# Beacon attention and low-rank mixer: every step of the script in another order, with score column groups in longer stretches

## The chip, the cores and the metric

The kernel runs on one core of one Trainium2 chip. The metric is the device time of one execution in microseconds (us), as the median of the runs. Three runs of the kernel before took 339.13, 339.48 and 340.19 us, with 339.48 us as the median.

## The reference

For 8 batches of 8 heads, 576 queries of 64 numbers attend to 16 beacon keys and to 576 keys under a causal mask. The heads are put side by side to 512 channels, and a mixer follows: a rank-32 product over the tokens, added to its input, and a two-layer ReLU network of 2,048 hidden channels, added again.

```python
k_all = np.concatenate([beacon_k, k], axis=2)
scores = scale * np.matmul(q, k_all.transpose(0, 1, 3, 2))
scores = np.where(causal, -1000000000.0, scores)
a = np.exp(scores - scores.max(-1, keepdims=True))
a /= a.sum(-1, keepdims=True) + 1e-09
x = np.matmul(a, v_all)                # then (batch, token, head * 64)
h = xt @ U @ V                         # xt: x with tokens last
u = x + h.transpose(0, 2, 1)
out = u + np.maximum(u @ w_ch1, 0.0) @ w_ch2
```

## The kernel before

The program is one straight list of steps. A string, SCRIPT, names them; `step` (a chain of comparisons on the first letter) turns each name into instructions, and every engine runs its instructions in exactly the order in which the script issues them. Nothing reorders them later: TensorE (PE), VectorE (DVE), ScalarE (ACT), GpSimd (POOL) and the DMA queues of SP and POOL each hold their own list, and only semaphores tie the lists together. So the order of the 961 names is the whole schedule.

Work is cut in pairs of heads, 32 of them, four for each batch. The steps of pair p are these, where a letter A or V after the name says whether ACT or DVE makes the copy:

- `k`, `q`, `b`, `v` and `w` issue the loads on POOL's queue. `H` and `G` regroup a loaded piece into a tile `pr` (L253 on DVE, L109 on ACT).
- `T` turns queries or keys so that the 64 numbers of a head lie along the partitions. In the first three batches PE does it (L261, L263, into PSUM) and a copy brings it to `qT` or `kT` (L109 on ACT, L264 and L265 on DVE). From pair 12 on, `R` issues the transposition as a DMA on SP's queue (tile `raw`, L283), and `T` is only the copy out of it.
- `Sa`, `Sb`, `Sc`, `Sd` are the four score column groups of a pair. Each has matmuls on 64 rows of the array, the two heads on the two halves (L316), and two exponentials on ACT (L321) that empty the two PSUM banks into `expt`. Group a is 496 columns wide, b 464, c 496 in three pieces, d 208. The number after a colon adds matmuls without use, which keep the array busy.
- `M` masks one head on DVE (L304, L306). `A` multiplies it with the values (15 matmuls, L331, tile `po`), then DVE divides by the row sums into `xb` (L339, L340). Four `expt` tiles hold two pairs at a time.
- `X` is the mixer's low-rank part for a batch: `X.0` works on 32-column tiles of the array (L371, then a copy on DVE, L377), `X.1` and `X.2` end in matmuls on 32 rows (L397). `x` issues DMA transpositions of `xb` that the later batches need for it.
- `g` is one of 16 first-layer units of a 512-token block (four matmuls of 512 columns, L529, evacuated by ACT at L533 and DVE at L534, or by ACT alone at L539). `p`, `P`, `F`, `V`, `N`, `W` and `U` make the two layers out of products of sums of blocks (L620 and L566 on PE, L601, L581 and L645 on DVE), and write the output.
- `I1` is one 512-column matmul without use (L241), 37 in all. `Z16` and `Z18` are one-element copies on POOL (L822) that read the DMA-transposed tile of pair 16 or 18: as POOL runs in order, the loads behind them are issued only when that tile has landed.

All PSUM tiles are taken in turn from one pool of 8 banks, so a new tile waits until an older one has been emptied by ACT or DVE. PE has three shapes of the array in this program besides the full one: 64 rows (`S`), 32 rows (end of `X.1` and `X.2`, and once in `e`), and 32 columns (`X.0`).

Of the kernel before, what the change touches and what calls it, by code (L numbers as in the profile page):

```python
# [27 lines left out]
def kernel(  # L28
# [760 lines left out]
    def step(t):  # L789
# [70 lines left out]
        GkV11 g0.1 M5.0 g0.10 g0.0 GkV8 g0.14 q2 g0.3 g0.11 GkA9 A5.0 A5.1 Sb7 I1 w11 TkV8 GqV8 GqV9 Sa7  # L860
        g0.2 M4.0 GqV11 Sd7 Sc7 TkV11 TkA9 g0.8 A4.1 M7.0 TqA9 A4.0 p00.0 p00.1 Sb6 v1B Sa6:0 g0.12
        p00.2 TqV11 M7.1 Sc6 g0.4 Sd6 g0.15 M6.0 GkA10 w20 U0.1 M6.1 TqV8 g0.6 A7.1 A7.0 Sd9 Sc9 w21
        A6.1 g0.7 A6.0 Sd8 g0.5 Sc8 Sa8 GqV10 X1.0 v2 b3 p01.0 p01.2 X1.1 P02.0 p01.1 X1.2 W0 P01.0 Sb8
        W4 W5 W1 Sb9 Sa9 W2 U1.1 W6 P01.1 TkA10 P02.1 M8.1 M9.0 TqA10 W7 b4 M8.0 U0.3 P05.0 P05.1 q3
        P06.0 P06.1 M9.1 A8.1 A9.0 A8.0 Sa10 P03.0 P03.1 k3 g1.15 A9.1 q4 Sa11 Sd10 g1.5 g1.1 Sb10 Sc10
        g1.3 g1.2 GkV13 GqA12 M10.0 GkA12 W3 P07.0 M10.1 P07.1 GqA13 Sb11 Sd11 GqA14 Sc11 M11.1 g1.9
        M11.0 GkA14 g1.12 A10.0 g1.7 g1.10 g1.0 R12 R13 R14 g1.6 TkV12 TqV12 TkV13 P04.0 GqA16 A11.1
        g1.8 U1.0 U1.3 TqA13 GkA15 P04.1 g1.14 A11.0 k4 A10.1 Sa13 Sd12 g1.11 p10.0 g1.4 GqA17 g1.13
        Sa12 Sb12 Sc12 p11.0 GqV15 X2.0 M12.0 P11.0 GkA17 P11.1 U1.2 X2.1 GkV16 p11.1 R15 P12.0 P12.1
        R16 P16.0 TqV14 Sd13 Sb13 M12.1 p10.1 p10.2 Sc13 P16.1 b5 U2.2 M13.0 TkA14 v3 A12.1 q5 A12.0 R17  # L870
        GkA19 P15.0 P15.1 p11.2 Sa14 Sd14 Sc14 x12 P17.0 TkV15 M13.1 P13.0 U2.3 A13.0 Sb14 Z16 M14.0
        P17.1 P13.1 GqA19 GqA18 TkV16 TqA16 A13.1 g2.13 g2.10 TqV17 TqV15 M14.1 v4 g2.4 Sa15 k5 Sc15
        TkA17 P14.0 A14.0 P14.1 A14.1 Sd16 GqV20 Sb15 Sd15 M15.1 GkV18 g2.0 x14 Sc16 M15.0 g2.7 g2.5
# [5 lines left out]
        GkV23 TkV20 TkA21 R22 b7 A19.1 g3.7 A19.0 R23 g3.13 g3.8 g3.5 Sa21 Sb21 Sc21 P24.0 P24.1 A18.1
        A18.0 Sb20 U3.3 Sd21 Sa20 M21.1 M21.0 g3.3 g3.2 Sc20 Sd20 X4.0 g3.4 M20.0 k6 GkV24 M20.1 g3.15  # L880
        GqA26 N5 v5 TkV22 g3.12 A21.0 U3.1 A20.0 g3.10 N1 GkA26 g3.1 x17 q7 g3.0 A20.1 TqV22 TqA23 TkV23
        g3.6 g3.14 g3.9 p30.0 p30.2 A21.1 Sc23 GkV25 p31.0 Sb23 GqV25 Sa23 R24 p30.1 x18 P31.0 P31.1
        GkV27 P32.0 P32.1 TkA24 p31.1 Sc22 p31.2 U3.2 k7 Sd22 v6 Sa22 P36.0 P36.1 Sb22 x19 M22.1 Sd23
        M23.0 P35.0 R25 R26 M22.0 P35.1 X4.1 P37.0 P37.1 X4.2 GqV27 TqA24 TqA25 P33.0 U4.1 P33.1 TkA25
        P34.0 R27 g4.0 GqV28 A22.1 TkV26 GkA28 R28 M23.1 g4.11 GqV29 g4.2 g4.6 TqV26 A23.0 g4.10 A23.1
        Sd25 Sc25 A22.0 g4.4 GkV29 R29 Sb25 GkV30 Sa25 M25.0 Sd24 TqV27 P34.1 TkA27 g4.3 U4.3 TkV28
        M25.1 g4.15 g4.13 g4.9 Sc24 Sa24 x21 Sb24 M24.0 U4.2 X5.0 A25.0 M24.1 g4.8 g4.12 U4.0 GqV31 x22
        g4.1 p40.0 p40.1 GqA30 A25.1 g4.7 Sa27 Sb27 A24.1 g4.14 A24.0 g4.5 p41.0 GkV31 Sc27 x23 Sc26
        p41.2 p41.1 Sd26 P41.0 P41.1 Sa26 Sd27 M27.1 Sb26 P45.0 p40.2 P42.0 P42.1 P45.1 TkA29 x20 X5.1
        U5.3 A27.1 R30 TqV29 M27.0 P46.0 P46.1 P43.0 P43.1 g5.13 A27.0 M26.0 M26.1 Sd29 g5.11 X5.2 g5.4  # L890
        U5.1 TqV28 P47.0 g5.2 A26.1 TkA30 x27 P47.1 A26.0 N0 Sb29 Sc29 R31 N4 g5.6 N2 Sb28 Sa29 g5.0 x24
        P44.0 g5.15 TqA30 M29.1 P44.1 x25 Sd28 Sa28 v7 Sc28 M28.1 M28.0 A29.1 g5.7 g5.14 TkV31 g5.1 g5.5
        M29.0 A28.0 g5.3 N3 A28.1 Sb30 TqV31 Sa30 g5.10 A29.0 U5.0 g5.12 g5.9 x29 g5.8 N6 p51.0 p51.2
        X6.0 p50.0 Sb31 Sd30 p50.1 x26 p51.1 Sc31 P51.0 P51.1 Sd31 p50.2 Sc30 M30.0 M30.1 Sa31 M31.0 x28
        U5.2 P52.0 M31.1 P56.0 X6.1 P55.0 A31.1 V6.0 U6.1 V6.2 P56.1 A31.0 x31 P52.1 A30.1 A30.0 V6.1
        x30 P57.0 P55.1 P57.1 X6.2 X7.0 N7 P53.0 P53.1 U6.2 F61.3 X7.2 P54.0 P54.1 F62.3 F61.2 X7.1
        F66.3 F62.2 F61.0 F65.0 V6.3 F65.3 V7.0 F62.0 U7.2 F66.2 F65.1 F67.3 F63.3 F61.1 F66.0 F62.1
        F63.0 F64.3 F66.1 F65.2 F67.2 F71.3 F67.0 F75.0 F67.1 F63.1 U7.0 F71.0 V7.1 F64.0 U7.3 F63.2
        p61.0 V8.0 P61.0 V7.3 F64.2 F64.1 F76.0 F76.3 U7.1 p61.1 U6.3 p60.0 p60.1 p60.2 U6.0 P61.1 P62.0
        P62.1 P65.0 p61.2 P65.1 guard V7.2 P66.0 P66.1 P63.0 P63.1 F75.3 F72.0 F72.3 F75.2 F77.0 F73.0  # L900
        P67.0 P67.1 F73.3 F71.1 F71.2 F72.1 F72.2 F76.1 F76.2 F75.1 V8.2 V8.1 P64.0 P64.1 F77.1 F77.2
        V8.3 F81.0 F74.0 F73.1 F74.1 U8.2 F77.3 p70.0 p70.2 F74.2 sum F73.2 p71.0 P71.0 p70.1 F74.3
        p71.2 F85.1 p71.1 F81.1 P71.1 P72.0 P72.1 F85.3 P75.0 P75.1 P76.0 P76.1 P73.0 P73.1 F82.1 U8.1
# [125 lines left out]
```

## Time and profile before

| | |
|---|---|
| median of 3 runs | 339.48 us |
| the profiled execution, span | 338.5 us |
| PE busy | 328.5 us of 338.5 |
| DVE busy | 264.9 us |
| ACT busy | 227.9 us |
| POOL busy | 99.8 us |
| matmuls on PE | 3,527 |

The span is the time from the first to the last instruction of one profiled execution; it lies 0.9 us below the median of the runs. Starts are given from the beginning of the span. In lists of instructions the columns are start, length, engine, source line, operation, tile written and tile read, shapes and a count; a pair of square brackets tells how long the engine stood idle before, and what ended that. A matmul's length includes the time in which it runs through the array, so its neighbours overlap with it; what one costs PE is read from the distance between starts.

### The profile page before, as it was taken

Reading aid. Unit: us, or ns where it says so; the run is one execution under the profiler, and the core shown is the slowest. Engines: PE = TensorE matmul, PEld = TensorE weight load, DVE = VectorE, ACT = ScalarE, POOL = GpSimd, SP = SyncE. Lnnn points to the kernel's source line nnn. Section 1 sums busy time; section 2 is a strip of 40 time slices with the busy share of each in tenths; the row PEclk is TensorE's granted clock in tenths of the full one; section 3 lists DMA queues with packets and bytes.
Section 4 is the critical chain, followed back from the end, with each engine's and each line's share of the span. In section 5 each row is a group of like instructions: output and inputs, shape, how many; then the busy total and the mean of one; then the engine's idle time right before and its main releaser. Section 6 shows DMA issues by size and latency. Waiting matters only on the chain.

```text
span 338.5 us, 8950 instructions
## 1 busy us (share of the span) xinstructions
PE 328.5 (97%) x3527; PEld 228.3 (67%) x3527; DVE 264.9 (78%) x690; ACT 227.9 (67%) x494; POOL 99.8 (29%) x129
## 2 busy tenths in 40 slices
...
GB/s 177 221 195 194 126 155 198 134 162 171 168 191 170 167 190 147 114 154 189 171 117 132 179 151 134 68 128 100 48 64 159 95 2 63 80 0 95 5 79 129
DMA packets 135600, 44.17 MB, mean 130 GB/s; under 512 B 108384, under 2 KB 130912, under 8 KB 135552
## 3 DMA queue, kind: packets, MB, share of 16 engines
...
q14 instruction: 19, 0.16, 0.2%
...
## 4 chain that ended last, share of the span: by engine, by line
PE 69%; DVE 17%; DMA 6%; issue 3%; ACT 2%; SPq 1%; DVEq 0%; ACTq 0%
PE gps L529 21%; PE cpY L620 14%; PE cpD L620 7%; PE po L331 7%; PE sps L316 7%; DMA stm<-in_q_dram 4%; PE cpA L620 3%; PE fpY L566 3%; DVE gT L581 3%; DMA raw<-pr 3%; DVE ob L645 2%; DVE sT L601 2%; DVE uT L404 2%; PE fpD L566 2%; DVE xb L340 1%
## 5 line engine op out<-in xcount | busy, mean ns | idle before, releaser
L321 ACT ACTIVATE expt<-sps 128x496 f16<-128x496 f32 (+2 forms) x256 | 111.6, 538 | 16.1 <-PE sps L316 14.7
L529 PE MATMUL gps<-uT,w 128*128 128x512 f16 x384 | 91.8, 379 | 0.3 <-DVE ob L645 0.3
L620 PEld LDWEIGHTS <-gT 128*128 128x128 f16 x576 | 54.6, 98 | 10.5 <-issue 2.2
L529 PEld LDWEIGHTS <-w 128*128 128x128 f16 x384 | 34.4, 98 | 37.5 <-issue 2.5
L587 POOL TENSOR_SCALAR gT<-gT 128x512 f16<-128x512 f16 x12 | 17.8, 1495 | 105.6 <-DVE gT L581 89.0
L620 PEld LDWEIGHTS <-sT 128*128 128x128 f16 x432 | 40.9, 98 | 7.9 <-issue 2.0
L203 POOL DMA_DIRECT2D vs<-in_v_dram x50 | 40.6, 824 | 4.9 <-DMA w<-in_moe_w_ch_dram 2.5
L331 PEld LDWEIGHTS <-expt 128*128 128x128 f16 (+1 forms) x960 | 35.5, 98 | 9.5 <-DVE expt L304 1.5
L539 ACT ACTIVATE gT<-gps 128x512 f16<-128x512 f32 x48 | 29.7, 628 | 15.7 <-PE gps L529 15.2
L304 DVE TENSOR_TENSOR expt<-expt,bigmask 128x512 f16<-128x512 f16 x64 | 26.7, 418 | 17.1 <-ACT expt L321 17.1
L331 PE MATMUL po<-vs,expt 128*128 128x65 f16 (+1 forms) x960 | 38.1, 194 | 1.2 <-DVE expt L304 1.2
L620 PE MATMUL cpY<-wsum,gT 128*128 128x256 f16 x288 | 36.1, 273 | 0.0
L620 PE MATMUL cpD<-w,sT 128*128 128x256 f16 x288 | 35.5, 273 | 0.3 <-DVE sT L601 0.3
L316 PE MATMUL sps<-qT,kT 64*128 64x80 f16 (+4 forms) x384 | 34.6, 282 | 0.5 <-ACT kT L109 0.5
L340 DVE TENSOR_TENSOR xb<-po,rec 128x320 f16<-128x320 f32 x64 | 31.5, 492 | 2.2
L534 DVE SCALAR_TENSOR_TENSOR gT<-gps,gT 128x256 f16<-128x256 f32 x48 | 19.8, 420 | 15.1 <-ACT gT L533 14.9
L109 ACT ACTIVATE hP<-fpY 128x512 f32<-128x512 f32 x24 | 13.7, 598 | 23.0 <-PE fpY L566 18.8
L533 ACT ACTIVATE gT<-gps 128x256 f16<-128x256 f32 x48 | 19.4, 415 | 11.5 <-PE gps L529 11.0
L316 PEld LDWEIGHTS <-kT 64*128 64x128 f16 x384 | 14.0, 94 | 18.9 <-issue 10.1
L645 DVE TENSOR_TENSOR ob<-cpY,ut 128x512 f32<-128x512 f32 (+1 forms) x28 | 18.7, 667 | 6.0 <-PE cpY L620 6.0
L566 PEld LDWEIGHTS <-wf 128*128 128x128 f16 x192 | 18.6, 98 | 2.9 <-issue 0.7
L620 PE MATMUL cpY<-w,gT 128*128 128x256 f16 x144 | 17.7, 273 | 0.0
...
## 6 DMA issues: line engine op xcount, KB each, us to landing
...
```

Source lines behind the costliest of these rows:

```text
L203: nc.gpsimd.dma_start(out=dst[a : a + nq[j], j, :, :], in_=src[hs, ds(q0[j], nq[j]), :].rearrange("h p d -> p h d"))
L304: nc.vector.tensor_tensor(out=e4, in0=e4, in1=bigmask, op=ALU.min)
L316: nc.tensor.matmul(ps[i][:, ds(o, w)], kT[hp, c, ds(P * ch, P)], qT[hp, c, ds(qa, w)], start=True, stop=True,)
L321: nc.scalar.activation(out=ex[i][:, ds(PAD + SLOT * g, gw[g])], in_=ps[i][:, 0 : gw[g]], func=AF.Exp, scale=scale)
L331: nc.tensor.matmul(po[:, j, :], ex[0 : nk[c], ds(blk[(c, j)], P)], vs[0 : nk[c], ds(c * H * E + h * E, E)], start=(c == 0), stop=(c == j),)
L340: nc.vector.tensor_tensor(out=xb[:, h // 2, :, ds(D * (h % 2), D)], in0=po[:, :, 0:D], in1=r.broadcast_to([P, NT, D]), op=ALU.mult)
L529: nc.tensor.matmul(g, w1[:, cc, ts(dc, P)], uT[:, cc, ds(ring(t0), 512)], start=(cc == 0), stop=(cc == NCC - 1))
L534: nc.vector.scalar_tensor_tensor(out=gT[:, dc, H2:512], in0=g[:, H2:512], scalar=0.0, in1=gT[:, dc, 0:H2], op0=ALU.max, op1=ALU.subtract,)
L539: nc.scalar.activation(out=gT[:, dc, :], in_=g, func=AF.Relu)
L566: nc.tensor.matmul(ps[:, i, :], a[:, kk, ts(2 * mp + i, P)], b[:, kk, :], start=opens and i == 0 and kk == 0, stop=kk == 1, skip_group_che ...
L620: nc.tensor.matmul(ps[:, i, :], a[:, f, ds(P * i, P)], b[:, f, :], start=opens and i == 0 and f == 0, stop=f == NK - 1, skip_group_check=True,
L645: nc.vector.tensor_tensor(out=out, in0=ps[:, ii, :], in1=other, op=ALU.add)
```

## The change

The multiset of steps is the same, and so is all code outside the string. The names stand in another order. The steps that issue loads on POOL's queue keep their order among themselves, and so do those that issue transfers on SP's queue. `Z16` and `Z18` are not among those kept: `Z16` stood ahead of `v4` and `k5` and now stands behind them, `Z18` stood ahead of `q6`, `b7`, `k6` and `v5` and now stands behind them. Of the 37 `I1`, 13 stood ahead of the first `T`, and 20 do now.

```diff
     SCRIPT = """
-        HqA0 I1 GkA0 I1 I1 I1 GqA0 I1 I1 HkV0 u I1 I1 I1 GkV1 I1 B I1 I1 I1 TqA0 TkA0 I1 TkV1 I1 s v0A
-        Sd0 Sb0 Sa0:3 I1 GqV1 TqV1 GkV2 Sc0 I1 GqV2 v0B I1 I1 Sc1 Sb1 I1 M0.0 Sd1 M0.1 TqV2 TkV2 I1 A0.0
...
-        A1.1 Sd3 Sa3:1 w12 I1 Sb3 cV M2.1 GqV4 A2.1 b1 k1B TqV4 GkA5 Sc3 I1 GkV4 I1 M3.0 q1B eA GqV5
-        TkV4 I1 GkV7 TkA5 I1 w13 A2.0 Sd4 M3.1 I1 TqV5 A3.0 GkA6 b2 w10 I1 A3.1 k2 Sa4 I1 Sd5 GqV6 GqV7
-        TkA7 X0.0 X0.1 Sa5:0 X0.2 Sb4 TqV7 TqV6 Sc5 TkA6 v1A g0.9 Sc4 M4.1 Sb5 M5.1 U0.0 U0.2 g0.13
...
-        g2.2 A15.0 A15.1 x13 Sd17 Sb17 g2.9 U2.0 X3.0 b6 Sa16 X2.2 g2.3 x15 Sa17 Sb16 R18 R19 Z18 GkV20
-        M16.1 Sc17 M17.1 M17.0 g2.1 g2.6 g2.12 M16.0 g2.8 g2.15 A17.0 U2.1 TqA19 GqA21 TqA18 X3.1 A16.1
...
+        I1 I1 HkV0 I1 u I1 I1 v0A I1 I1 GkV1 v0B I1 I1 s I1 HqA0 B I1 I1 I1 I1 GqA0 I1 I1 GqV1 GkA0 q1A I1
+        I1 I1 I1 TqA0 k1A w12 TkA0 b1 TkV1 I1 I1 Sa0:3 I1 Sc0 Sd0 Sb0 I1 TqV1 I1 M0.0 I1 k1B GkV2 I1 Sd1
+        Sa1:2 M0.1 GqV2 TkV2 I1 Sc1 Sb1 TqV2 A0.1 M1.1 A0.0 I1 Sc2 q1B Sd2 Sa2:1 M1.0 GqV3 I1 GkV3 Sb2 GqV5
+        I1 GqV4 I1 I1 TqA3 M2.0 TkV3 I1 I1 M2.1 I1 A1.0 A1.1 Sc3 Sd3 TqV5 Sa3:1 Sb3 GkA5 cV w13 I1 A2.0
+        GkV4 A2.1 eA M3.1 b2 M3.0 TkA5 TkV4 TqV4 GkA6 GkV7 A3.0 TkA6 GqV6 A3.1 Sa4 Sa5:0 w10 k2 Sb5 X0.0
+        X0.1 X0.2 Sd5 Sc5 Sb4 GqV7 TqV6 v1A g0.8 M5.0 GkV11 Sc4 Sd4 M4.0 g0.9 TqV7 U0.0 TkA7 M4.1 g0.0 GkV8
+        g0.14 g0.1 M5.1 A5.0 g0.2 U0.2 q2 A5.1 Sb7 Sc7 Sa7 A4.0 g0.15 TkV8 A4.1 Sd7 g0.3 GqV9 Sd6 Sa6:0
...
+        R18 Sd17 Sc17 A16.1 R19 TkA18 M16.0 M17.1 g2.0 U2.1 g2.2 GkA21 g2.9 TkA19 TqA18 X3.2 g2.11 g2.13
+        A16.0 M17.0 A17.1 GqV20 X3.1 q6 TqA19 g2.7 g2.1 g2.4 p21.0 A17.0 P21.0 P21.1 GqA21 Sb18 Sb19 Sc18
...
     """
```

The first place is on PE, in the first-layer units of block 0, at group d of pair 6 (128x208). Before, it stood alone between two units of L529:

```order
L529 MATMUL gps<-uT,w_108 128x512
L316 LDWEIGHTS kT_125
L316 MATMUL sps_1155<-qT,kT_125 128x208
L316 LDWEIGHTS kT_125
L316 MATMUL sps_1156<-qT,kT_125 128x208
L529 LDWEIGHTS w_108
```

Now group a of the same pair (128x496) stands behind it:

```order
L529 MATMUL gps<-uT,w_108 128x512
L316 LDWEIGHTS kT_125
L316 MATMUL sps_1060<-qT,kT_125 128x208
L316 LDWEIGHTS kT_125
L316 MATMUL sps_1061<-qT,kT_125 128x208
L316 LDWEIGHTS kT_125
L316 MATMUL sps_1066<-qT,kT_125 128x496
L316 LDWEIGHTS kT_125
L316 MATMUL sps_1067<-qT,kT_125 128x496
L261 LDWEIGHTS hd_641
```

Counted through PE's whole list, the shape of the array changes 177 times before and 147 times now; the score groups stand in 68 stretches before and in 56 now. Up to `X0.0`, the first low-rank step, the changes are 36 before and 23 now.

The second place is on DVE, in the last stretch before `X0.0`. `expt_122` and `expt_123` are the two heads of pair 3, the last pair of batch 0. Before, the mask of `expt_122` stood 8 rows higher, and only that of `expt_123` was left here:

```order
L304 TENSOR_TENSOR expt_123<-expt_123,bigmask 128x4x128
L306 TENSOR_TENSOR expt_123<-expt_123,mask 80x80
L264 COPY qT<-tps 128x64
L265 COPY qT<-tps 128x512
L339 RECIPROCAL rec<-po 128x5
L340 TENSOR_TENSOR xb<-po,rec 128x5x64
```

Now both masks stand together, with the copies of keys and queries of pair 4 behind them, and the divisions of pair 3 behind those:

```order
L304 TENSOR_TENSOR expt_123<-expt_123,bigmask 128x4x128
L306 TENSOR_TENSOR expt_123<-expt_123,mask 80x80
L304 TENSOR_TENSOR expt_122<-expt_122,bigmask 128x4x128
L306 TENSOR_TENSOR expt_122<-expt_122,mask 80x80
L264 COPY kT_125<-tps 128x80
L265 COPY kT_125<-tps 128x512
L264 COPY qT<-tps 128x64
L265 COPY qT<-tps 128x512
L253 COPY pr<-st_245 128x512
L339 RECIPROCAL rec<-po 128x5
L340 TENSOR_TENSOR xb<-po,rec 128x5x64
```

So both heads of pair 3 are now masked late, and four more rows of DVE stand between the masks and the `xb` that `X0.0` reads.

The third place is on ACT, ahead of `X3.1`. Before, these rows were:

```order
L533 ACTIVATE gT<-gps 128x256 x2
L539 ACTIVATE gT<-gps 128x512 x3
L109 ACTIVATE qT<-raw 128x512
L109 ACTIVATE pr<-st_2120 128x512
L109 ACTIVATE qT<-raw 128x512
```

Now they are:

```order
L109 ACTIVATE kT_124<-raw 128x512
L533 ACTIVATE gT<-gps 128x256 x2
L109 ACTIVATE pr<-st_2044 128x512
L539 ACTIVATE gT<-gps 128x512
L109 ACTIVATE kT_124<-raw 128x512
L109 ACTIVATE qT<-raw 128x512
L539 ACTIVATE gT<-gps 128x512 x2
```

A copy out of `raw` has moved in front of the unit evacuations, and two of them stand between the evacuation of `g2.9` and that of `g2.11`. `X3.1` takes four PSUM banks on PE soon after `g2.11` and `g2.13`, and waits for ACT there.

More of the change, by code (lines that the diff above doesn't have):

```diff
@@ L859 @@
-        TkA7 X0.0 X0.1 Sa5:0 X0.2 Sb4 TqV7 TqV6 Sc5 TkA6 v1A g0.9 Sc4 M4.1 Sb5 M5.1 U0.0 U0.2 g0.13
[L860 to L873, printed above, removed]
@@ L879 @@
[L879 to L893, printed above, removed]
@@ L894 @@
[L894 to L903, printed above, removed]
@@ new lines @@
+        GkA9 TkV11 M7.0 g0.11 Sc6 Sb6 GqV8 g0.13 TqV8 w11 M6.1 M6.0 g0.10 M7.1 GkA10 v1B GqV11 g0.4 g0.6
+        w20 g0.12 p00.0 U0.1 A7.1 A6.0 TqA9 A7.0 w21 v2 GqV10 TkA9 A6.1 p00.2 g0.5 Sd9 Sc9 TqV11 TqA10 g0.7
+        b3 TkA10 Sb8 X1.0 p01.0 X1.2 X1.1 Sa8 p01.1 p00.1 p01.2 W0 P01.0 P02.0 W4 W1 W5 W2 P01.1 W6 Sc8 Sa9
+        Sd8 U1.1 b4 P02.1 Sb9 P05.0 U0.3 P05.1 q3 M8.1 P06.0 P06.1 GqA14 M9.0 M9.1 P03.0 P03.1 g1.1 A9.1
+        g1.9 W7 k3 GqA12 GkA12 A8.1 q4 GkA14 A9.0 M8.0 g1.14 GqA13 P07.0 GkV13 W3 g1.5 A8.0 g1.4 g1.15 R12
@@ new lines @@
+        g1.7 R13 Sd10 Sc11 Sc10 R14 P07.1 g1.2 U1.0 TkV12 Sa10 Sb10 TkV13 M10.1 P04.0 U1.3 g1.11 GqV15 Sd11
+        Sb11 Sa11 GkA15 P04.1 TqV14 g1.0 TqA13 M10.0 TqV12 GqA16 g1.3 g1.13 M11.0 GqA17 k4 g1.10 g1.8 GkA17
+        g1.12 A10.0 U1.2 A10.1 R15 M11.1 g1.6 A11.0 p11.0 TkA14 GkV16 p10.0 Sb12 Sd12 Sa12 P11.0 A11.1
+        P11.1 Sc12 Sc13 Sb13 X2.0 GqA18 M12.0 R16 b5 p11.1 p11.2 p10.1 P16.0 GkV18 M12.1 P12.0 X2.1 U2.2 v3
+        P16.1 A12.1 q5 Sa13 R17 Sd13 p10.2 A12.0 TqA16 TqV15 M13.1 P17.0 P15.0 M13.0 TkV16 Sd14 Sb14 P15.1
@@ new lines @@
+        A13.1 P17.1 TkA17 TkV15 x12 P12.1 GkA19 A13.0 U2.3 P13.0 P13.1 GqA19 Sa14 Sd15 Sc14 v4 k5 M14.0
+        TqV17 P14.0 P14.1 M14.1 Sb15 Sa15 Sc15 M15.1 g2.12 A14.0 g2.10 g2.14 A14.1 M15.0 g2.8 Sc16 Sd16
+        Sb16 x14 Z16 A15.1 A15.0 GkV20 x13 U2.0 g2.15 X2.2 X3.0 Sa16 Sb17 Sa17 b6 x15 M16.1 g2.5 g2.6 g2.3
+        R18 Sd17 Sc17 A16.1 R19 TkA18 M16.0 M17.1 g2.0 U2.1 g2.2 GkA21 g2.9 TkA19 TqA18 X3.2 g2.11 g2.13
+        A16.0 M17.0 A17.1 GqV20 X3.1 q6 TqA19 g2.7 g2.1 g2.4 p21.0 A17.0 P21.0 P21.1 GqA21 Sb18 Sb19 Sc18
@@ new lines @@
+        GkV23 p20.0 P22.0 P22.1 p20.1 p21.1 R20 P26.0 GkV22 P26.1 R21 Sd18 Sa18 GqA23 U3.0 p20.2 GqV24
+        P25.0 GqA22 P27.0 P25.1 p21.2 M18.1 Sa19 Sc19 Sd19 P27.1 P23.0 TkV20 x16 TqV20 N1 TkA21 M19.1 M19.0
+        P23.1 A18.1 g3.13 M18.0 g3.9 A19.1 R22 g3.14 g3.1 TqA21 A18.0 g3.10 GqV27 b7 P24.0 A19.0 Sa20 Sd20
+        Sc20 R23 P24.1 U3.3 k6 g3.0 v5 Z18 N5 U3.1 g3.6 Sb20 Sc21 Sb21 M20.0 TkV23 GkV24 x17 g3.2 g3.5 Sd21
+        Sa21 M20.1 M21.1 TkV22 g3.8 TqV22 g3.4 g3.15 A20.0 g3.3 GkV27 TqA23 q7 GkA26 R24 g3.7 M21.0 g3.11
@@ new lines @@
+        x18 GqV25 U3.2 GkV25 TqA24 p30.0 A21.1 GqA26 P31.0 k7 A20.1 g3.12 A21.0 P31.1 v6 p31.0 x19 Sd22
+        p30.1 Sb23 X4.0 p31.2 Sc23 Sb22 R25 p31.1 P36.0 p30.2 P32.0 R26 P32.1 X4.2 TqA25 P36.1 P35.0 P35.1
+        Sa22 X4.1 P37.0 P37.1 GkV29 Sa23 Sc22 Sd23 U4.1 P33.0 GqV29 TkA24 P33.1 M22.1 g4.9 R27 GqV28 M23.0
+        M22.0 M23.1 g4.14 g4.4 A22.0 TkA25 A23.0 TkV26 A22.1 GkA28 A23.1 N2 R28 g4.12 TqV26 Sa25 Sb24 P34.0
+        g4.1 GkV30 g4.5 R29 Sa24 Sd25 Sb25 P34.1 g4.6 Sd24 Sc24 Sc25 U4.3 M24.0 g4.2 M24.1 g4.0 GkV31 M25.1
@@ new lines @@
+        g4.11 M25.0 A24.0 N4 g4.15 GqV31 x21 g4.13 U4.2 TkV28 TqV27 A24.1 g4.10 U4.0 GqA30 x22 A25.0 x23
+        g4.7 g4.3 TkA27 g4.8 A25.1 Sd26 Sa26 X5.0 Sb26 Sc26 Sb27 p40.0 P42.0 p41.0 p40.1 p41.2 TqV29 P41.0
+        P41.1 M26.0 x20 Sa27 Sc27 Sd27 p41.1 P42.1 M26.1 N0 M27.1 p40.2 P46.0 P45.0 P45.1 M27.0 P46.1 X5.1
+        A26.1 U5.3 N3 TkA29 A27.1 R30 TqV28 P43.0 P43.1 A26.0 A27.0 g5.5 g5.3 N6 U5.1 g5.1 P47.0 x27 R31
+        Sa28 Sa29 Sc29 P47.1 x24 g5.2 g5.15 g5.4 g5.12 TqA30 TkV31 TqV31 g5.13 N7 Sb29 Sd29 Sd28 P44.0
@@ new lines @@
+        M29.1 P44.1 g5.14 TkA30 M29.0 X5.2 Sc28 x25 v7 g5.7 A29.0 g5.0 g5.6 U5.0 A29.1 Sa31 Sb28 Sc31 x29
+        p51.0 M28.1 p51.1 M28.0 g5.8 p51.2 g5.9 g5.10 g5.11 A28.0 A28.1 Sb31 Sc30 Sd31 X6.0 p50.0 p50.1
+        P51.0 P51.1 x26 x28 Sd30 Sa30 Sb30 M31.0 p50.2 P52.0 M31.1 A31.0 P56.0 M30.0 M30.1 X6.1 U5.2 P55.0
+        P55.1 A31.1 A30.1 P56.1 U6.1 x31 V6.0 A30.0 P52.1 V6.1 P57.0 x30 X7.0 X6.2 P57.1 P53.0 X7.2 P53.1
+        F65.2 U6.2 P54.0 X7.1 P54.1 V7.0 F65.3 V6.2 F61.3 F65.0 F61.0 F62.3 V7.1 F61.2 F66.3 V6.3 F62.0
```

18 lines of the change are left out of this document (10 added, 8 removed).

## The prediction

> **What bounds the kernel now.** I read the page's shares first, then PE's waits, then the lists of instructions at the places that the change touches.
>
> ```profile
> PE 328.5 (97%) x3527; PEld 228.3 (67%) x3527; DVE 264.9 (78%) x690; ACT 227.9 (67%) x494; POOL 99.8 (29%) x129
> ```
>
> PE is busy 97% of the span, so its own work sets the time unless somebody makes it wait. The view of waits, for PE alone, has these rows in the first 60 us (first four) and behind them (last three); columns are the time in total, how often, and the longest:
>
> ```profile
> PE idle L241 <- POOL ident masks.py:199: 1.6, 1, 1.6
> PE po L331 <- DVE expt L304: 1.2, 1, 1.2
> PE tps L261 <- DVE hd L741: 0.6, 1, 0.6
> PE sps L316 <- ACT kT L109: 0.5, 1, 0.5
> ...
> PE fpD L566 <- DVE ob L645: 0.5, 1, 0.5
> PE cpD L620 <- DVE sT L601: 0.3, 1, 0.3
> PE gps L529 <- DVE ob L645: 0.3, 1, 0.3
> ```
>
> That is 2.3 us of waiting after the start in the first 60 us and 1.1 us in the remaining 278. The old order has almost no idle time left to win. What it can win is PE time that counts as busy. What it can lose is this near absence of waits.
>
> **What the change saves: changes of the array's shape.** The timeline of PE, around two stretches of units at L529:
>
> ```profile
> 34.57 1.02 PE L529 MATMUL gps<-uT,w 128*128 128x512 f16 x4
> 35.53 0.58 PE L316 MATMUL sps<-qT,kT 64*128 64x336 f16 x8
> 36.05 6.22 PE L529 MATMUL gps<-uT,w 128*128 128x512 f16 x28
> 42.10 1.08 PE L331 MATMUL po<-vs,expt 128*128 128x65 f16 x30
> ```
>
> From 36.05 to 42.10, 28 matmuls of one shape take 6.05 us, 0.216 us each, so four take 0.864. The four that begin at 34.57 are followed by score groups, on 64 rows, after 0.96: the change costs 0.096 us. The way back: a 512-column matmul at 0.216 gives 0.42 ns a column, the two heads of a group run side by side, and groups c and b (496 and 464 columns) make 0.405 us; from 35.53 to 36.05 it took 0.52, so 0.11. I take 0.098 us for one change. The order has 177 of them before and 147 now: 30 x 0.098 = **2.9 us saved**. All matmuls stay, 37 idle ones among them. This saving is certain as PE work; whether it reaches the end depends on what PE waits for. The Trainium skill, page "TensorEngine Tiling (Array Packing)", section "Key Properties", says that a change of tiling mode drains the engine, but not a change of tile within a mode; the rows agree, with 0.1 us for it.
>
> **The start gives much of it back.** 23 changes of shape stand ahead of `X0.0` (L371) where 36 stood: 13 of the 30, 1.3 us, are saved where PE has been waiting. What decides there is the chain over ACT and DVE:
>
> ```profile
> 1.59 5.50 PE L241 MATMUL idle<-ident 128*128 128x512 f16 x13 [1.59 <-POOL ident masks.py:199]
> 6.92 0.20 PE L261 MATMUL tps<-ident,hd 80*128 80x80 f16 x1
> 11.14 0.82 PE L241 MATMUL idle<-ident 128*128 128x512 f16 x3
> 11.90 0.58 PE L316 MATMUL sps<-qT,kT 64*128 64x336 f16 x8
> 30.44 0.59 PE L371 MATMUL qtp<-xb,Usb 128*32 128x128 f16 x20
> ...
> 9.07 5.71 ACT L321 ACTIVATE expt<-sps 128x208 f16<-128x208 f32 x14 [0.35 <-PE sps L316]
> 18.96 4.74 ACT L321 ACTIVATE expt<-sps 128x464 f16<-128x464 f32 x10
> 24.75 1.06 ACT L321 ACTIVATE expt<-sps 128x496 f16<-128x496 f32 x2 [0.54 <-PE sps L316]
> ```
>
> 13 idle matmuls fill 1.59 to 6.92, and the first `T` follows at once. Now 20 stand there. Later ones take (11.90 - 11.14 - 0.1) / 3 = 0.22 us, so seven more put the first `T` at 8.4, 1.5 us later. The first exponential stood 2.15 us behind it; the wider group a is now first, so I put it at 10.7. Fourteen exponentials take 5.71 us and ten 4.74, so a pair's eight take about 3.4. In the old order ACT ran from 9.07 to 25.81 through four pairs.
>
> The DVE rows give pitches, from start to start:
>
> ```profile
> 23.05 0.40 DVE L304 TENSOR_TENSOR expt<-expt,bigmask 128x512 f16<-128x512 f16 x1
> 23.38 0.18 DVE L306 TENSOR_TENSOR expt<-expt,mask 80x80 f16<-80x80 f16 x1
> 23.49 0.28 DVE L253 COPY pr<-st 128x512 f16<-128x512 f16 x1
> 24.81 0.18 DVE L264 COPY qT<-tps 128x64 f16<-128x64 f16 x1
> 24.91 0.68 DVE L265 COPY qT<-tps 128x512 f16<-128x512 f16 x1
> 25.51 0.28 DVE L253 COPY pr<-st 128x512 f16<-128x512 f16 x1
> 29.21 0.18 DVE L339 RECIPROCAL rec<-po 128x5 f32<-128x5 f32 x1
> 29.42 0.49 DVE L340 TENSOR_TENSOR xb<-po,rec 128x320 f16<-128x320 f32 x1
> 29.83 0.18 DVE L339 RECIPROCAL rec<-po 128x5 f32<-128x5 f32 x1
> ```
>
> A mask costs 0.44, a copy of queries or keys 0.70, a division 0.62, a regrouping 0.2. I walk the new order by hand with these. The pairs' exponentials end at 14.1, 18.0 (0.4 waited for a copy of keys behind a regrouping) and 21.4. Pair 3 then needs its keys on DVE, behind the mask of pair 2: 21.4 + 0.44 + 0.70 and PE's part put its first exponential at 23.1 and its last end at 26.5, against 25.81. DVE comes to pair 3's masks at 27.6, because two divisions, a copy of queries, three casts (1.1 us) and two more divisions stand ahead. From there, as the second place in the section on the change shows: two masks, two copies, two regroupings, two divisions, 0.9 + 1.4 + 0.4 + 1.2 = 3.9. So `X0.0` begins at about 31.6 where it began at 30.44: 1.2 later. Of the 1.3 saved by then, 0.7 is spent on steps that now also stand ahead of it (two idle matmuls, groups a and b of pair 5 and a turn, for groups d of pairs 4 and 5 and a turn: 1.1 against 0.46), and 0.6 has been counted as gain. The start costs **1.8**. Bounds: 0, if ACT ends at 25.1 (10.7 plus 14.4, the old 16.7 less its waits and a regrouping) and DVE is in time; 3.2, if the full 1.5 of the late first `T` arrives on top of my walk's 1.7.
>
> Right behind, both pairs 4 and 5 stand around `X0`, with five L529 units (4.3 us) between them and `A5.1` where eight were. ACT has 16 exponentials (7.2), four copies of `uT` (1.4), a copy of keys and a unit (1.3) from 31.3 on, so 41.2, then DVE masks twice: 42.3. PE, with its own work from 31.6, is there at 41.4: **1.0** of waiting, between 0 and 2.
>
> **Later stretches.** The third place, ahead of `X3.1`. In the old order ACT's rows there read:
>
> ```profile
> 127.00 2.91 ACT L321 ACTIVATE expt<-sps 128x496 f16<-128x496 f32 x6
> 132.33 1.11 ACT L109 ACTIVATE qT<-raw 128x512 f16<-128x512 f16 x1
> 133.33 0.63 ACT L109 ACTIVATE pr<-st 128x512 f16<-128x512 f16 x1
> 133.85 1.09 ACT L109 ACTIVATE qT<-raw 128x512 f16<-128x512 f16 x1
> 134.83 0.59 ACT L539 ACTIVATE gT<-gps 128x512 f16<-128x512 f32 x1
> ```
>
> In the new one, from the first exponential of `Sa16` to the evacuation of `g2.11`, ACT has ten exponentials (4.3), five half units (0.38 each, 1.9), three copies out of `raw` (1.0 each), a regrouping (0.5) and two units (1.1): 10.8 us. PE has 9.8 from the end of `Sa16` to `X3.1`, which needs the bank of `g2.11`: it waits **1.1**, between 0 (PE already late) and 2. The Trainium skill, same page, section "PSUM Bottleneck", warns that tiling speeds up TensorE but not the emptying of PSUM; a pair of heads' group takes PE 0.2 us here and ACT two exponentials of 0.47, so this place is such a case.
>
> The other long stretches I cost together. Three groups fill six of eight banks, and what PE does next hides ACT's 2.8 us if it brings its own evacuations to DVE. The third place shows what it costs where it doesn't. For all of them I take **0.7**, two thirds of one such wait, between 0 and 3. Of the 1.1 us of late waits in the old order I let **0.4** go, since other steps stand there now.
>
> **DMA.** POOL's rows of the old order:
>
> ```profile
> 108.10 0.21 POOL L822 COPY gate<-raw 1x1 f16<-1x1 f16 x1 [9.26 <-DMA raw<-pr]
> 129.42 0.18 POOL L822 COPY gate<-raw 1x1 f16<-1x1 f16 x1 [13.48 <-DMA raw<-pr]
> ...
> raw<-pr SPq DMA_TRANSPOSE x20, 4.7
> ```
>
> The two gates held POOL for 9.3 and 13.5 us, and with it the loads of values and keys of batches 4 and 5 and of queries of batch 6. Now those are issued without them, earlier, beside the transpositions of pairs 16 to 19, which land 4.7 us after issue in the median. I cost it at nothing: the copies that need them stand behind 10 us of ACT's and DVE's own work. With that cover gone it is the last rival below.
>
> **The sum** goes on the median, since the profiled execution lies 0.9 below it: -2.9 + 1.8 + 1.0 + 1.1 + 0.7 - 0.4 = +1.3, so 339.48 + 1.3 = **340.8 us**, 0.4% slower. Its own range, from the start at 0.7 to 3.2 and the places around it, is 339.6 to 342.6.
>
> **Rivals.**
>
> 1. The saving arrives. Mechanism: in the stages behind the start, PE is the only bound (1.1 us of waits in 278), ACT's late start is caught up by the 1.7 us that it idled in the old order, and long stretches are covered. Then -2.9 with 0.3 to 1.5 of waits: 336.9 to 338.1, say 337.6. For it: PE's 97%. Against it: the slack at the start is already in my walk, and 13 of 30 changes lie there. It decides where `X0.0` stands at 30.4 or earlier.
> 2. Nothing to tell: start 1.8, late places 1.0, so -0.1; 338.6 to 340.4, within 0.3%, which is about what a measurement of this kernel can tell from no change.
> 3. Loads without gates. If transpositions of pairs 16 to 19, or of pair 23, whose turn now follows 3 us behind its issue and not 16, land as late as a crowded queue makes them, then copies out of `raw` block ACT or DVE in order, and PE behind them. The slowest of the old 20 took 10.3 us, 5.6 above the median:
>
> ```profile
> DMA to landing us min/median/max: 3.1/4.7/10.3
> ```
>
> One such landing, taken in full, adds 2.5 to 5 to my sum, so 343.3 to 345.8. Against it: ACT's queue hides a few us each time.
>
> **Chances.** My forecast 0.46, the first rival 0.24, the second 0.16, the third 0.14. Faster by over 0.3% is the first rival and a bit of others: 0.25. Within 0.3% (338.5 to 340.5) takes the second rival and the lower part of my own range: 0.26. Slower 0.49. The range that should hold 8 in 10 goes from 337.3 to 343.6.
>
> **What would show it.** Right on the saving: PE's busy time of unchanged groups falls in no row, but changes between shapes still cost 0.1 each. Right on the start: first `T` at 8.4, first exponential near 10.7, L371 first at 31 to 32, and waits of L371 and L331 on DVE. Right on the third place: a wait of L397 on ACT near 130 us. Wrong: L371 at 30.4 or before, or PE waits of under 3 us in all, or waits on copies out of `raw`.

## The result, and the profile after

The changed order takes 353.17 us (median of 4 executions, 349.78 to 356.33), the order before 339.64 us (4 executions, 339.13 to 340.19). The ratio is 1.0304, with a 95% interval of 1.0269 to 1.0339. The four executions of the changed order stand in two groups, 349.78 and 350.67, and 355.67 and 356.33; the ratio and the profile are from the lower one, and where a kernel below shows such groups, its ratio is too. The profiled span is 348.1 us, 9.6 above the 338.5 of before.

The prediction was 340.8 us, in a range from 337.3 to 343.6. It had the sign and not the size.

The page's row of shares, then the view of waits for PE behind the first 60 us, in the changed order:

```profile
PE 330.7 (95%) x3527; PEld 229.4 (66%) x3527; DVE 262.8 (75%) x690; ACT 226.5 (65%) x494; POOL 99.6 (29%) x129
```

```profile
PE gps L529 <- DVE xb L340: 4.1, 1, 4.1
PE cpD L620 <- DVE ob L645: 2.1, 1, 2.1
PE sps L316 <- ACT expt L321: 1.2, 2, 1.0
PE ups L397 <- ACT gT L539: 0.3, 1, 0.3
```

The old order had 1.1 us of waits there. Now there are 7.7, and 7.4 of them are in three places that my sum doesn't contain. The engine in a row is only the last link, though. What DVE and ACT themselves waited for at two of them stands in their own timelines (DVE first):

```profile
166.28 0.29 DVE L253 COPY pr<-st 128x512 f16<-128x512 f16 x1 [6.69 <-DMA raw<-pr]
166.49 0.19 DVE L339 RECIPROCAL rec<-po 128x5 f32<-128x5 f32 x1
166.71 0.49 DVE L340 TENSOR_TENSOR xb<-po,rec 128x320 f16<-128x320 f32 x1
```

```profile
113.24 1.08 ACT L109 ACTIVATE kT<-raw 128x512 f16<-128x512 f16 x1 [5.21 <-DMA raw<-pr]
```

Both waited for a DMA transposition (L283). The chain of waits, in order of time, shows how long each was under way:

```profile
104.32 8.89 DMA raw<-pr
...
156.39 9.87 DMA raw<-pr
```

and the timeline of POOL shows what had been issued just ahead of them:

```profile
98.00 4.19 POOL L203 DMA_DIRECT2D vs<-in_v_dram  x5
102.16 0.91 POOL L196 DMA_DIRECT2D st<-in_k_dram  x1
103.03 0.71 POOL L190 DMA_DIRECT2D hd<-in_k_dram  x1
103.70 0.18 POOL L822 COPY gate<-raw 1x1 f16<-1x1 f16 x1
...
150.69 5.21 POOL L203 DMA_DIRECT2D vs<-in_v_dram  x5
155.88 0.18 POOL L822 COPY gate<-raw 1x1 f16<-1x1 f16 x1
156.00 0.88 POOL L196 DMA_DIRECT2D st<-in_q_dram  x1
```

At 104.32 `R17` is issued behind `v4` and `k5`, whose gate `Z16` now comes after them, at 103.70. At 156.39 `R22` is issued behind `v5` and the first piece of `q7`. It could not go earlier because SP's queue was held by an output write until 155.88, as SP's rows show:

```profile
155.88 0.38 SPq L648 DMA_DIRECT2D out_dram<-ob  x1
156.39 6.01 SPq L283 DMA_TRANSPOSE raw<-pr  x2
```

And the step that waits for `R22` isn't a copy out of `raw`: it is the regrouping `GqV27`, six steps behind it in the script, which writes a `pr` buffer that the transposition still reads. The divisions behind it on DVE release the `po` banks that PE's next unit needs.

The third place is near 70 us. Here the late transfer is `U0.3`, which turns `uT` for the output, and the rows are from the timeline of all engines:

```profile
61.59 0.73 POOL L190 DMA_DIRECT2D hd<-in_q_dram  x1
61.77 1.26 SPq L520 DMA_TRANSPOSE ut<-uT  x1
...
70.01 0.69 DVE L645 TENSOR_TENSOR ob<-cpD,ut 128x512 f32<-128x512 f32 x1 [2.58 <-issue]
```

The trace has its landing at 69.93, 8.2 us after issue, and DVE starts 0.1 later.

Two of the three waits cost more than their length. PE's granted clock, by stretches (columns: the stretch, its length, busy time and count for PE, PEld, DVE, ACT and POOL, then PEclk):

```profile
114.00:117.00 3.00, 1.87 (x11) 0.72 (x9) 0.00 (x0) 3.00 (x8) 1.36 (x2) 1.00 0.42 156
117.00:121.00 4.00, 3.83 (x28) 2.02 (x27) 2.55 (x9) 3.99 (x9) 0.27 (x1) 0.57 1.12 130
...
163.00:167.00 4.00, 0.19 (x1) 0.00 (x0) 0.68 (x3) 0.84 (x3) 0.00 (x0) 1.00 1.46 164
168.00:172.00 4.00, 4.00 (x19) 1.46 (x18) 2.45 (x8) 3.52 (x8) 0.00 (x0) 0.57 0.59 178
```

A mean of 0.57 over 4 us is 4 x 0.43 = 1.7 us of work lost each time, or 3.4 us at half clock (from 118 to 120 us, and from 169 to 171, the granted clock is 0.50). So by the waits the three places cost an estimated 2.1, 1.2 + 1.7 = 2.9, and 4.1 + 1.7 = 5.8 us: **10.8** together, more than the whole 9.6. The section on the loads measures the three directly, at 12.0.

### The profile page after: what moved, and what is told of

The parts are those of the page before. It is cut to its first block, busy times and chain, and to the rows that moved or that the text cites. A ratio compares the mean times of both kernels' runs of the same rounds, so it can differ in the third digit from the quotient of the medians.

```text
span 348.1 us, 8936 instructions
## 1 busy us (share of the span) xinstructions
PE 330.7 (95%) x3527; PEld 229.4 (66%) x3527; DVE 262.8 (75%) x690; ACT 226.5 (65%) x494; POOL 99.6 (29%) x129
## 4 chain that ended last, share of the span: by engine, by line
PE 75%; ACT 12%; DMA 5%; DVE 4%; issue 2%; SPq 0%; POOL 0%; ACTq 0%; POOLq 0%
PE gps L529 19%; PE cpY L620 17%; PE cpD L620 8%; ACT expt L321 7%; PE fpY L566 6%; PE po L331 6%; PE sps L316 6%; DMA raw<-pr 5%; PE cpA L620 4%; PE fpD L566 3%; PE idle L241 2%; PE fpA L566 2%; ACT pr L109 1%; ACT kT L109 1%; DVE xb L340 1%
## 5 line engine op out<-in xcount | busy, mean ns | idle before, releaser
L321 ACT ACTIVATE expt<-sps 128x496 f16<-128x496 f32 (+2 forms) x256 | 110.3, 548 | 14.7 <-PE sps L316 13.2
L529 PE MATMUL gps<-uT,w 128*128 128x512 f16 x384 | 93.3, 385 | 4.2 <-DVE xb L340 4.1
L529 PEld LDWEIGHTS <-w 128*128 128x128 f16 x384 | 35.4, 99 | 42.3 <-DVE xb L340 4.6
L620 PEld LDWEIGHTS <-gT 128*128 128x128 f16 x576 | 54.1, 98 | 11.1 <-issue 3.5
L620 PE MATMUL cpY<-wsum,gT 128*128 128x256 f16 x288 | 36.8, 273 | 0.0
L316 PE MATMUL sps<-qT,kT 64*128 64x80 f16 (+4 forms) x384 | 35.4, 286 | 1.5 <-ACT expt L321 1.2
L316 PEld LDWEIGHTS <-kT 64*128 64x128 f16 x384 | 14.3, 95 | 20.3 <-issue 12.7
L620 PE MATMUL cpA<-w,gT 128*128 128x256 f16 x144 | 18.2, 273 | 0.1
```

The source lines that it names most:

```text
L316: nc.tensor.matmul(ps[i][:, ds(o, w)], kT[hp, c, ds(P * ch, P)], qT[hp, c, ds(qa, w)], start=True, stop=True,)
L321: nc.scalar.activation(out=ex[i][:, ds(PAD + SLOT * g, gw[g])], in_=ps[i][:, 0 : gw[g]], func=AF.Exp, scale=scale)
L529: nc.tensor.matmul(g, w1[:, cc, ts(dc, P)], uT[:, cc, ds(ring(t0), 512)], start=(cc == 0), stop=(cc == NCC - 1))
L620: nc.tensor.matmul(ps[:, i, :], a[:, f, ds(P * i, P)], b[:, f, :], start=opens and i == 0 and f == 0, stop=f == NK - 1, skip_group_check=True,
```

## The experiments

Each was run beside the kernel before on one chip. In the diffs, names stand in the order of the script. The theory throughout is **late landings**: a transposition issued behind loads lands late, and the new order puts the first step that needs it too close. The rival is **long stretches**: the new order overloads ACT and DVE.

| run | median, us | ratio to before (95%) | profiled span |
|---|---|---|---|
| changed order | 353.17 | 1.0304 (1.0269 to 1.0339) | 348.1 |
| ut_early | 354.98 | 1.0366 (1.0302 to 1.0429) | 354.4 |
| r17_early | 347.44 | 1.0219 (1.0183 to 1.0256) | 345.3 |
| r22_early | 349.26 | 1.0315 (1.0267 to 1.0363) | 346.9 |
| three_early | 346.20 | 1.0208 (1.0174 to 1.0241) | 341.8 |
| few_loads_after | 338.86 | 0.9974 (0.9953 to 0.9994) | 336.7 |
| few_loads_before | 339.18 | 0.9975 (0.9957 to 0.9993) | 336.9 |
| gates_old | 348.54 | 1.0228 (1.0168 to 1.0289) | 346.2 |
| before_gates_moved | 345.72 | 1.0182 (1.0135 to 1.0229) | 343.1 |
| few_loads_start_old | 339.72 | 0.9981 (0.9958 to 1.0003) | 337.9 |
| hybrid_tail | 338.38 | 0.9945 (0.9924 to 0.9967) | 336.4 |
| mended | 345.40 | 1.0124 (1.0076 to 1.0172) | 351.9 |
| slack | 345.26 | 1.0115 (1.0079 to 1.0150) | 344.1 |

### One late transfer issued earlier

```diff
# ut_early
-Sb9 P05.0 U0.3 P05.1 q3
+Sb9 P05.0 P05.1 q3
-p00.0 U0.1 A7.1
+p00.0 U0.1 U0.3 A7.1
# r17_early
-q5 Sa13 R17 Sd13
+q5 Sa13 Sd13
-M12.0 R16 b5
+M12.0 R16 R17 b5
# r22_early
-g3.9 A19.1 R22 g3.14
+g3.9 A19.1 g3.14
-Sd20 Sc20 R23 P24.1
+Sd20 Sc20 P24.1
-P25.0 GqA22 P27.0
+P25.0 GqA22 R22 P27.0
-x16 TqV20 N1
+x16 TqV20 R23 N1
```

Expected of the first:

> The changed order with one step moved: U0.3, the transfer of ut that landed 8.2 us after issue behind the loads of queries and keys of batch 3, now directly behind U0.1, some 24 us earlier. Late landings as the cause: PE's 2.1 us wait of L620 cpD for DVE ob near 70.8 us is gone and the span falls by about 2.2 us, from 348.1 to 346. Rival, long score stretches as the cause (ACT and DVE simply too busy): DVE comes to the same place late by its own work, PE waits there for at least 1 us still, and the span falls by less than 0.7 us.

Of the second:

> The changed order with R17 moved directly behind R16, so that this transposition is issued near 98.5 us and not at 104.3, ahead of most of the loads of values and keys. Late landings: ACT's 5.2 us wait for raw is under 1 us, PE's waits of L316 for ACT near 116 us (1.2 us, with the slow matmuls behind them 2.9 us) are gone, span near 345.2. Rival, long stretches: ACT is behind by its exponentials, PE still waits for ACT there for 1 us or more, span above 347.4.

Of the third:

> The changed order with R22 moved directly behind GqA22 and R23 directly behind TqV20, ahead of the output write that held SP's queue until 155.9 us. Late landings: DVE's 6.7 us wait (a regrouping into pr whose buffer the transposition still reads) falls under 1 us, PE's 4.1 us of L529 at 163 to 167 us and the slow matmuls behind it (1.6 us) are gone, span near 342.3. Rival, long stretches: less than 2 us of it comes back.

`r17_early` did what late landings said: the waits of L316 for ACT near 116 us are gone with the half clock behind them, and the span is 345.3 for the 345.2 expected. That it agrees to 0.1 is luck. PE runs the same list of matmuls as in the changed order, so the starts can be compared one by one: the moved place gave back 3.9 and not 2.9, the place near 70 us gave back 0.9 with nothing moved, and the place near 163 us cost 1.5 more, where the half clock lasted from 162.3 to 169.1.

In `ut_early` the 2.1 us wait near 70 us is gone as well; by the starts of the matmuls, 2.2 us came back there. But the profiled execution was the longest of its four and shows 4.0 us of L316 waiting for ACT and 5.1 us of L529 waiting for DVE, so its span says nothing. The ratio doesn't fall. Inconclusive on the time, and in part on the place too: in `r22_early`, where `U0.3` wasn't moved, it landed after 5.1 us and cost nothing either.

`r22_early` lost the 4.1 us wait, and only 1.2 us of span came back where 5.8 were expected. By the number the rival was right. By the rows it wasn't. Compared matmul by matmul, the moved place gave back 5.9, and 2.2 and 2.1 more came back near 70 and 117 us; the start took 0.9, a new place from 90 to 98 us took 4.0, and two from 176 to 191 us took 4.4. The first new place stands before the first moved step, and there too the wait is for landings. DVE near 90 us:

```profile
86.16 0.68 DVE L291 COPY kT<-raw 128x512 f16<-128x512 f16 x1 [2.56 <-DMA raw<-pr]
88.64 0.72 DVE L291 COPY kT<-raw 128x512 f16<-128x512 f16 x1 [1.79 <-DMA raw<-pr]
92.56 0.60 DVE L291 COPY qT<-raw 128x512 f16<-128x512 f16 x1 [1.95 <-DMA raw<-pr]
```

Up to there this kernel's instructions are the same as the changed order's, whose profile has no such wait at that place: `R12` to `R14` landed 9.6 to 11.1 us after issue here, and 5.7 to 7.3 there. So which landing is late differs from one execution to the next, and one mend alone can't be priced by one span.

### All three

> All three moves together. Late landings: the three gains add, about 10.9 us, so span near 337.2 and time near 338.9, within 0.4% of the kernel before. Rival, long stretches: above 344 us, with PE waits for ACT and DVE at other places in place of the three.

The span was 341.8, between the two theories, but it is the shortest of the six executions. The median is 346.2, about 344.5 of span: by the number the rival was right here too. PE's longest waits behind 60 us in that shortest one:

```profile
PE sps L316 <- ACT expt L321: 1.7, 1, 1.7
PE ups L397 <- ACT gT L539: 0.5, 1, 0.5
PE gps L529 <- DVE xb L340: 0.4, 1, 0.4
```

The three places are gone or small. The 1.7 is ACT again standing in front of a copy out of `raw`, this time for pair 25: it waits 6.9 us there until 183.73. Other landings take the place of some of the mended ones.

### The loads taken away

The test that doesn't depend on which landing is late leaves out most of the loads, in both orders.

```diff
     def k_loads(b, L, hs):
-        main_load(nc.gpsimd, k[b], L[1][0][:, hs, :], hs)
+        ms = slice(0, 2) if isinstance(b, int) and b > 2 else hs
+        main_load(nc.gpsimd, k[b], L[1][0][:, ms, :], ms)
...
-        regroup(Ls[b], c, i, copy, prs[p])
+        regroup(Ls[b], c if b < 3 else 0, i, copy, prs[p])
...
-                v_loads(v[b], beacon_v[b], vss[b % 2], hs)
+                if b < 3:
+                    v_loads(v[b], beacon_v[b], vss[b % 2], hs)
```

Queries are treated like keys.

> The changed order; of queries and keys of batches 3 to 7 only the first two heads are loaded for the tokens behind the first 80 rows (all pairs use these), and values of batches 3 to 7 are not loaded, so that POOL's queue moves 0.4 MB a batch and not 1.8. All other work is kept. Late landings as the cause: transpositions have nothing to land behind, no wait on raw over 1 us, the half-speed stretches of PE are gone, and the span is 336 to 338. Rival, long score stretches that overload ACT and DVE: the span stays above 344.

> The old order with the same loads left out. Late landings: it has little to win, 337.5 to 338.5 of span, and so the changed order without these loads is 0 to 2 us faster than this one, where with them it is 9.6 slower. Rival, long stretches: the distance between the two orders stays at 6 us or more.

The two orders now take 338.86 and 339.18 us, ratios to the kernel before of 0.9974 and 0.9975. The spans are 336.7 and 336.9; the second is 0.6 below the range expected. The whole difference between the orders hangs on the loads, and long stretches alone don't slow the changed order. PE's waits behind 60 us, in the changed order with few loads (two lines have been added ahead, so L399 is L397 of the page):

```profile
PE ups L399 <- ACT gT L541: 0.2, 1, 0.2
```

With and without the loads, PE runs the changed order's 3,527 matmuls in the same order, so the start of each can be compared in the two profiles. With the loads PE loses 2.2 us between 66 and 71 us, 3.9 between 113 and 122, and 5.9 between 162 and 174. That is 12.0 at the three places, 0.1 elsewhere, and the start is 0.9 earlier: 11.3 of the 11.4 us between the spans. The old order loses 1.6 by its loads: 1.0 before `X0.0`, 0.4 near 92 us and little else.

The transpositions of the changed order land so, from issue, without the loads:

```profile
DMA to landing us min/median/max: 3.0/3.4/5.7
```

and so with them:

```profile
DMA to landing us min/median/max: 3.1/5.8/9.9
```

`R22` lands after 3.8 us and not 9.9, though the same output write stands 0.5 us ahead of it on SP's queue: the write isn't what delays it. The old order with its loads had 3.1, 4.7 and 10.3. It has landings as late as the changed one. Its 10.3 us is even the same transposition, `R22`, issued at 150.69. But there nobody needed it yet: the first copy out of it stands 36 steps later, and `GqV27` 97 (36 and 6 in the changed order).

### The gates alone

One part of the change undone, and the same part done alone:

```diff
# gates_old
-Sd15 Sc14 v4 k5 M14.0
+Sd15 Sc14 Z16 v4 k5 M14.0
-GqV20 X3.1 q6 TqA19
+GqV20 X3.1 Z18 q6 TqA19
-Sb16 x14 Z16 A15.1
+Sb16 x14 A15.1
-g3.0 v5 Z18 N5
+g3.0 v5 N5
# before_gates_moved
-Sb14 Z16 M14.0
+Sb14 M14.0
-Sa15 k5 Sc15
+Sa15 k5 Z16 Sc15
-R19 Z18 GkV20
+R19 GkV20
-N5 v5 TkV22
+N5 v5 Z18 TkV22
```

> The changed order with only Z16 put back ahead of v4 and k5, and Z18 ahead of q6. Gates as the cause (my third rival in the prediction): v4 and k5 are issued some 5 us later, pair 17's transposition lands within 6 us, ACT's 5.2 us wait falls to 1 to 2, span about 345.5; the waits near 70 and 163 us stay. Any transposition behind any load, gate or not: less than 1.5 us comes back. Long stretches: nothing comes back.

> The old order with only Z16 moved behind v4 and k5, and Z18 behind v5. Gates as the cause: the loads of batch 4 and 5 overtake the transpositions of pairs 16 to 19, and the old order loses 2 to 5 us (341 to 345). If the slack of each transposition counts and not the gates: within 1 us of the kernel before, since the copies stand 9 us and more behind R16 and R17 in the old order.

`gates_old`: span 346.2 (345.5 expected), with no wait of L316 for ACT near 116 us; the waits of the other two places are still there, 4.5 us near 163 and 1.2 near 70. `before_gates_moved`: 345.72 us, ratio 1.0182, a little more than the 2 to 5 us expected. The old order loses 6 us by two one-element copies that stand elsewhere. In the profile all of it is lost between 112 and 122 us, so at `Z16`; the move of `Z18` cost nothing there. The rows, POOL first, then SP, DVE and PE:

```profile
97.85 4.20 POOL L203 DMA_DIRECT2D vs<-in_v_dram  x5
105.52 0.88 POOL L196 DMA_DIRECT2D st<-in_k_dram  x1 [3.48 <-ACT expt L321]
```

```profile
103.98 3.67 SPq L283 DMA_TRANSPOSE raw<-pr  x1
```

```profile
115.97 1.09 DVE L291 COPY qT<-raw 128x512 f16<-128x512 f16 x2 [4.43 <-DMA raw<-pr]
```

```profile
117.12 0.60 PE L316 MATMUL sps<-qT,kT 64*128 64x496 f16 x8 [4.40 <-DVE qT L291]
```

`v4` is issued from 97.85 on, where the gate had held the same transfers until 109.15. `R17`, issued at 103.98, lands 12.0 us later and not 3.9, and DVE had come to the copy 7.6 us after the issue (115.97 - 4.43 - 103.98). So the slack that I had credited to the old order is worth nothing once the gate is gone.

### The start, the tail, and more mends

`few_loads_start_old` puts the old start in front of the changed order, with few loads (`TkA6`, `Sa5:0` and `Sb5` stay ahead of `X0.0`, as in the changed order); `hybrid_tail` is the old order up to `v7` and the changed one behind it, with all loads. Both keep the multiset of steps.

> The changed order with few loads (as in few_loads_after), but up to X0.0 the steps stand as in the old order, and behind it the remaining ones in the changed order; 161 changes of shape and not 147. My prediction's term (the new start costs 1.8 us in all that the change of order does there): X0.0 is earlier by 1 us, PE's waits in the first 40 us fall by about 2 us, 14 changes of shape cost 1.4 us, so the time is 0.4 to 1.0 us below few_loads_after. Rival (the new start costs nothing, X0.0 stood at 29.5 to 30.4 in all runs of it): the 14 changes show alone, 0.5 to 1.4 us above few_loads_after.

> All loads as in the reference. The old order up to v7, the last load (step 718 of 961), and what is left in the changed order. Late waits: the old order has 1.6 us of PE's waits behind 260 us (0.5 of L620 for DVE, 0.6 of L566 for DVE, 0.3 at 325 us) and the changed one 0.3, and no transposition of queries and keys is left to be late, so 1 to 1.3 us faster than before: ratio 0.996 to 0.997. If the tail's waits follow from the steps ahead and not from its order: no difference, ratio 0.999 to 1.001.

The old start doesn't help. The ratio to before is 0.9981 with it and 0.9974 without, the span 337.9 and 336.7, and `X0.0` stands at 30.45 and 30.35. The gain that my term promised isn't there. The rival, that the new start costs nothing, fits the spans; by the ratios the two can't be told apart.

`hybrid_tail` is faster than both kernels: 338.38 us, ratio 0.9945 (0.9924 to 0.9967), a little more than expected. The view of waits has no wait of PE behind 60 us there. Its transpositions land no earlier than in the changed order:

```profile
DMA to landing us min/median/max: 3.1/6.0/13.2
```

Two more mends of the changed order. `mended` has the three moves, `R25` directly behind `GkV25`, and both gates at their old places. `slack` moves the first users and not the transfers:

```diff
# slack (and U0.3 as in ut_early)
-A13.1 P17.1 TkA17 TkV15
+A13.1 P17.1 TkV15
-Sa15 Sc15 M15.1
+Sa15 Sc15 TkA17 M15.1
-A18.0 g3.10 GqV27 b7
+A18.0 g3.10 b7
-Sb21 M20.0 TkV23 GkV24
+Sb21 M20.0 GkV24
-x18 GqV25 U3.2
+x18 GqV25 GqV27 TkV23 U3.2
```

> The changed order with all loads, U0.3, R17, R22 and R23 early as in three_early, R25 moved directly behind GkV25 as well, and Z16 and Z18 back ahead of v4 and q6. Late landings: the 6.9 us wait of ACT near 184 us in three_early goes too, PE's waits behind 100 us fall under 2 us, span 339 to 341, 3 to 5 us below three_early's median. Rival: a crowded queue delays some other transposition each time, and the time stays within 1.5 us of three_early's 346.2.

> The changed order with all loads; no transposition of queries and keys is moved, but the first steps that wait for them: TkA17 from directly behind P17.1 to behind Sc15 (38 steps behind R17 and not 16), GqV27 and TkV23 to behind GqV25 (51 and 40 steps behind R22 and R23, not 6 and 14), and U0.3 early as in ut_early. Slack as the cause, since R22 and R23 landed as late in the old order (10.3 and 9.1 us) and nobody waited there: the waits near 70, 113 and 163 us go, span 338 to 341. Rival, the crowded queue hits other copies in their place: span 344 or more.

Ratios of 1.0124 and 1.0115: about three fifths of the loss comes back in each, and not all of it. In both it is the rival's number that came: `mended` is within 1.5 us of `three_early`, and the profiled span of `slack` is 344.1, just past the 344 named, with executions from 341.00 to 350.23. In `slack` the places near 70, 113 and 163 us are gone, as expected; the largest wait is a new one, again behind a copy out of `raw`:

```profile
88.97 1.57 DVE L291 COPY kT<-raw 128x512 f16<-128x512 f16 x2 [4.83 <-DMA raw<-pr]
```

In `mended` the profiled execution was the longest of seven and shows 3.6 us behind ACT and 3.6 behind DVE, so only its time counts. So late landings cause the loss, but giving the known ones more distance isn't enough: others show. That the changed order can be repaired in full with its own sequence of score groups was not shown.

## Why the prediction was wrong, step by step

**The step that failed** is "DMA. ... I cost it at nothing: the copies that need them stand behind 10 us of ACT's and DVE's own work." With few loads the two orders are equal, and with all loads the changed one is 3% slower: what the new order loses, it loses by landings behind the loads. Three things were wrong in that step. Work on the same engine is no cover when the copy stands in that engine's queue: everything behind it waits too. I looked for copies out of `raw`, but the largest wait was a regrouping into the buffer that a transposition reads, and another was an output sum. And I had seen the gates go (they held POOL for 9.3 and 13.5 us in the old order) without asking what they protected; alone they are worth 6 us there.

**The third rival** had the mechanism, and with pairs 16 to 19 it named one of the late landings, that of pair 17. Pair 23, which it also named, wasn't waited for; pair 22's was, and not by a copy. It got a chance of 0.14, and a price of one landing, 2.5 to 5 us. There were three, and two of them brought 1.7 us of half clock each. The sign of "wrong" that I named, waits on copies out of `raw`, came at one of the three places.

**The saving** was right. Over PE's whole list the distance from start to start at a change of shape exceeds the matmul's own columns by 0.099 us in the median before and 0.098 after, 177 and 147 times. With few loads the excess at changes falls from 19.3 to 16.1 us, 3.2 for the 2.9 predicted, and all other excess rises by 3.0. So the order itself gives back what it saves, as the sum said in kind; it said +1.3 and the spans say -0.2.

**The start** was half right. The first `T` stood at 7.3 to 8.7 us in the nine profiles with the new start (8.1 in the mean, 8.4 predicted) and at 5.8 to 7.0 in the four of the old order up to `X0.0` and beyond. But `X0.0` stood at 29.5 to 30.8 (30.2 in the mean) against 29.4 to 30.4 (29.8): later by 0.5 and not by 1.2, so that the start costs about 1.1 (the 0.5, and the 0.6 of gain that the sum had counted already) for the 1.8 in the sum. The profile of before had the latest of its group and the profile after the earliest of its own, so that this pair alone shows `X0.0` 1.0 earlier (PE's timeline after; the first row are the idle matmuls):

```profile
1.59 5.90 PE L241 MATMUL idle<-ident 128*128 128x512 f16 x20 [1.59 <-POOL ident masks.py:199]
7.32 0.20 PE L261 MATMUL tps<-ident,hd 80*128 80x80 f16 x1
...
29.48 0.76 PE L371 MATMUL qtp<-xb,Usb 128*32 128x128 f16 x20 [0.27 <-ACT expt L321]
```

That is no merit of the order: the first 13 idle matmuls took 5.50 us before, 0.42 each, and the 20 after 5.90, 0.30 each. Behind `X0.0` the changed order takes 10.6 us more than the old one. There the order itself gives -1.1 (the same stretch with few loads), the three places 12.0 and other places 0.1, less the 0.6 that the loads cost the old order: 10.4 of the 10.6.

**A5.1 and the third place** were over-sized. At `A5.1` the view of waits has no row for PE, where 1.0 was predicted. `X3.1` did wait for ACT, as a row of the view above shows (L397, 0.3 us), for the 1.1 predicted. **The late waits** of the old order were under-sized: of the 1.1 us I let 0.4 go, and the changed order has none of them left. They aren't the loads' doing, since the old order with few loads still has waits of 0.5 and 0.3 us there; in `hybrid_tail`, with the changed order's tail, they are gone.

**Why a range to 343.6 wasn't wide enough:** the price of a late landing had no upper bound in it. Two such landings at the slowest less the median, 5.6 us each by the row that I quoted, would have given 351 to 352, inside what was measured. That this sum comes near is partly luck: it holds two landings and no half clock, and there were three.
